# A gated recurrence with a mixer behind it: three of four batches loaded as whole tensors and computed in whole chunks

## The chip, the core and the metric

The kernel runs on one core of a Trainium2 chip. The metric is the time of one execution in device microseconds. Five engines work side by side, each through a queue of its own in the order in which the program wrote it: TensorE (PE in the profile; the loading of its weights is shown as PEld), VectorE (DVE), ScalarE (ACT), GpSimd (POOL) and SyncE (SP), which here issues all DMAs. An instruction that has to wait holds up what stands behind it on its engine.

## What is computed

The inputs are fp32: q, k, v and alpha of 4 batches, 8 heads, 768 tokens, 48 elements; U (768 x 32), V (32 x 768), w1 (384 x 1536) and w2 (1536 x 384). The output is 4 x 768 x 384 in fp32.

```
for t in range(S):                                   # S = 768, per batch and head
    state = alpha[t][:, None] * state + outer(k[t], v[t])
    y[t] = q[t] @ state
x = y, with the 8 heads side by side                 # 768 x 384 per batch
u = x + ((x.T @ U) @ V).T                            # low-rank mixing over tokens
out = u + relu(u @ w1) @ w2                          # MLP, 384 -> 1536 -> 384
```

## The kernel before

**The pieces.** Tokens are cut into chunks of C = 128, NC = 6 of them in a batch. In a chunk the decay is turned into sums of logarithms: ScalarE takes Ln of alpha (`lt`), TensorE sums it over the tokens by a triangular matrix, ScalarE takes exp of plus and minus the sum (`aa`, `ai`), q and k are multiplied by these (`rq`, `rk`) and transposed (`qT`, `kT`), and then the chunk's output is a masked product of scores (`pm`) with v (`rv`, a bf16 copy), plus q times the state (`st`) of the chunks before. A state update follows.

Two functions do this. `stage_gla` (L541) takes a chunk of 128 tokens with all 8 heads. `stage_pair` (L361) takes a block of 256 tokens with 4 heads: a partition holds two neighbouring tokens of each head, and the unit is done as two sub-chunks on halves of TensorE's rows. Either has six units in a batch. `PAIR = (0, 1, 2)` (L214) says which batches use pairs: the first three. In `stage_gla` the products `rq` and `rk` and the cast `rv` are given to GpSimd alone; in `stage_pair` the products may go to VectorE too, and the cast to ScalarE.

After a batch's six units comes `stage_mix` (L673: x.T U at L681, the residual's product with V at L712, transposes at L722), then the MLP: `mlp1` (first half, L749, two token halves of 12 tiles with three matmuls each) and `mlp2` (second half, L772, six chunks of 12 matmuls), whose sum is stored by SP (L780) from one of four `ou` buffers.

**The loads.** Each input of each unit has its own 192 KB tile from the pool `io`, with 36 slots (L261). A pair's tile is read in pieces of 2 x 48 elements, 384 B (L342), a chunk's in pieces of 48, 192 B (L349). w1 and w2 come in 12 tiles each through the same slots, and are cast to bf16 by GpSimd or ScalarE. A slot comes free when its reader is done.

**What sets the order.** All steps are entered with `P.add`: the engines that may do it and its cost on each in ns, what it reads and writes, and a key `prio`. `Plan.run` (L89) then walks through time by these costs. It takes, for an engine, the step that can start first, and among steps that can start at the same moment the one with the smallest key; it gives out the buffer slots as it goes, and writes each engine's queue in the resulting order. The chip runs the queues in this order whatever the steps really take. For a DMA the plan adds its cost to a common clock of the data, and lets SP run up to 3500 ns ahead of it; a pair load is entered with 750 ns, a chunk load with 1000, a weight tile with 540, a store with 550.

The keys of attention are 100 x (6 b + unit) and a little more, so 0, 600, 1200 and 1800 on for batches 0 to 3. The MLP's are 100 x (6 (b + 1) + 3 + 6 x), where x goes from 0 to 0.5 in the first half and from 0.5 to 1 in the second: 900 to 1500 for batch 0, 1500 to 2100 for batch 1. Loads have a unit's number 6 b + unit as their key, with offsets: alpha 0.7 earlier, v up to 1.25 later. U and V have 2.5, w1 5.5, w2 7.9 (`W2AT`).

Before the data come, TensorE is kept busy by `filler` matmuls (until 28 us of the plan).

Of the kernel before, what the change touches and what calls it, by code (L numbers as in the profile page):

```python
# [8 lines left out]
FP32 = mybir.dt.float32  # L9
BF16 = mybir.dt.bfloat16  # L10
AF = mybir.ActivationFunctionType
# [3 lines left out]
class Pool:  # L15

    def __init__(self, slots):
        self.slots = list(slots)
        self.free = [0.0] * len(self.slots)


class Buf:
# [10 lines left out]
    def __call__(self):  # L33
        return self.slot
# [140 lines left out]
def mm(*cols):  # L175
    return sum(max(c / 2.4 + 2.5, 25.0) for c in cols)
# [3 lines left out]
def kernel(  # L180
# [24 lines left out]

    const = ctx.enter_context(tc.tile_pool(name="const", bufs=1))
# [3 lines left out]
    def slots(name, n, shape, dtype):  # L210
        return [const.tile(shape, dtype, name=f"{name}{i}") for i in range(n)]

    W2AT = 7.9
    PAIR = (0, 1, 2)  # L214
    RES = (1, 1, 1, 0)
    P = Plan()
    nc.scalar.preload_act_table_set("natural_log_exp_and_others")

    u_in = const.tile([128, NC, R], FP32, name="u_in")
    v_in = const.tile([R, S], FP32, name="v_in")  # L220
    v_bf = const.tile([R, S], BF16, name="v_bf")
    u_sb = const.tile([128, NC, R], BF16, name="u_sb")
    vm_sb = const.tile([128, S], BF16, name="vm_sb")
# [23 lines left out]
    sel = const.tile([R, 4, R], BF16, name="sel")  # L247
# [10 lines left out]
    nc.vector.memset(offd[0:64, :, 1], -30000.0)  # L258
    nc.vector.memset(offd[64:128, :, 0], -30000.0)

    io = Pool(slots("io", 36, [C, H, D], FP32))  # L261
    lt_s = slots("lt", 3, [C, H, 64], BF16)
    rq_s = slots("rq", 3, [C, H, 64], BF16)
    rk_s = slots("rk", 4, [C, H, 64], BF16)
# [12 lines left out]
    pms = Pool(slots("pm", 3, [C, HP, 2, C], BF16))  # L277
    sms = Pool(slots("sm", 2, [128, DM], FP32))
    sts = Pool(slots("st", 4, [128, HP, 2 * D], BF16))
    xbs = Pool(slots("xb", 3, [128, NC, DM], BF16))  # L280
    ubs = Pool(slots("ub", 3, [128, NC, DM], BF16))
    utxs = Pool(slots("utx", 2, [128, DM], BF16))
    uts = Pool(slots("uT", 3, [128, NCT, S], BF16))
    h1s = Pool(slots("h1t", 2, [128, NJ, S], BF16))
    outs = Pool(slots("ou", 4, [C, DM], FP32))

# [9 lines left out]
    def copy(eng, dst, src):  # L296
        if eng == "ACT":
            nc.scalar.copy(dst, src)  # L298
        elif eng == "DVE":
            nc.vector.tensor_copy(dst, src)  # L300
        else:
            nc.gpsimd.tensor_copy(dst, src)  # L302

    def small():
        P.add({"SP": 450.0}, lambda e: nc.sync.dma_start(u_in, moe_U.rearrange("(c p) r -> p c r", p=128)), w=["u_in"], prio=2.5)
        P.add({"SP": 500.0}, lambda e: nc.sync.dma_start(v_in, moe_V), w=["v_in"], prio=2.5)
        P.add({"POOL": 300}, lambda e: nc.gpsimd.tensor_copy(u_sb, u_in), r=["u_in"], w=["u"], prio=395)
        P.add({"POOL": 800}, lambda e: nc.gpsimd.tensor_copy(v_bf, v_in), r=["v_in"], w=["v_bf"], prio=396)
        for i in range(2):
            vb = Buf(bank)  # L310
            sl = slice(i * TW, (i + 1) * TW)
            P.add({"PE": mm(TW)}, lambda e, vb=vb, sl=sl: nc.tensor.matmul(vb()[:, 0:TW], lhsT=sel.rearrange("r a b -> r (a b)"), rhs=v_bf[:, sl], start=True, stop=True), r=["v_bf"], w=[vb], prio=397, mode="V")
            P.add({"DVE": 470, "ACT": 390}, lambda e, vb=vb, sl=sl: copy(e, vm_sb[:, sl], vb()[:, 0:TW]), r=[vb], w=[("vm", i)], prio=398)

    def weight(dst, src, key, prio, pr, engs):
        t = Buf(io)
        P.add({"SP": 540.0}, lambda e: nc.sync.dma_start(flat(t), src), w=[t], prio=prio)  # L317
        P.add(engs, lambda e: copy(e, dst, flat(t)), r=[t], w=[key], prio=pr)

    def flat(t):  # L320
        return t().rearrange("p h d -> p (h d)")

    def weights1():
        for g in range(4):
            cs = slice(g * DM, (g + 1) * DM)
            for ct in range(NCT):
                weight(w1_sb[:, ct, cs], moe_w_ch1[ct * 128 : (ct + 1) * 128, cs], ("w1", g, ct), 5.5 + 0.01 * g, 560 + g, {"POOL": 485})
# [6 lines left out]
    tiles = {}  # L334

    def stage_loads(b):
        def load(t, src, c, key):
            if b in PAIR:
                hs, sl = slice((c % 2) * HP, (c % 2 + 1) * HP), slice((c // 2) * 2 * C, (c // 2 + 1) * 2 * C)
                P.add(  # L340
                    {"SP": 750.0},
                    lambda e: nc.sync.dma_start(  # L342
                        t().rearrange("p (h j) d -> p h (j d)", j=2), src[b, hs, sl, :].rearrange("h (p j) d -> p h (j d)", j=2)
                    ),
                    w=[t], prio=key,
                )
                return
            sl = slice(c * C, (c + 1) * C)
            P.add({"SP": 1000.0}, lambda e: nc.sync.dma_start(t(), src[b, :, sl, :].rearrange("h t d -> t h d")), w=[t], prio=key)  # L349

        for c in range(NC):
            at, qt, kt, vt = (Buf(io) for _ in range(4))
            tiles[b, c] = at, qt, kt, vt
            kk = b * NC + c
            for t, src, o in ((at, alpha, -0.7 if c else 0.0), (kt, k, 0.1), (qt, q, 0.2), (vt, v, 1.25 if c < NC - 1 and b in PAIR else 0.3)):
                load(t, src, c, kk + o)

    def xk(b, xb, c):
        return [(xb, c, 0), (xb, c, 1)] if b in PAIR else [(xb, c)]

    def stage_pair(b, u, sprev, xb):  # L361

        blk, half = u // 2, u % 2
        pr = (b * NC + u) * 100.0
        sl = 0.0 if b == 0 else 150.0
        at, qt, kt, vt = tiles[b, u]

        def raw(t):
            return t().rearrange("p (h j) d -> p j h d", j=2)

        def jh(x):
            return x.rearrange("p (j h) d -> p j h d", j=2)

        lt = Buf(lts)
        P.add({"ACT": 435}, lambda e: nc.scalar.activation(jh(lt()[:, :, 0:D]), raw(at), AF.Ln), r=[at], w=[lt], prio=pr + 40, slack=sl)  # L375
        rv = Buf(rvs)
        P.add({"POOL": 480, "ACT": 420}, lambda e: copy(e, jh(rv()), raw(vt)), r=[vt], w=[rv], prio=pr + 20, slack=sl)

        cb = Buf(bank)
        Q = HP * D  # L380
# [16 lines left out]
        aa, ai, tot = Buf(aas), Buf(ais), Buf(tots)  # L397
# [10 lines left out]
        P.add(both, lambda e: f_scale(e, rk, kt, ai), r=[kt, ai], w=[rk], prio=pr + 10, slack=sl)  # L408
        P.add(both, lambda e: f_scale(e, rq, qt, aa), r=[qt, aa], w=[rq], prio=pr + 11, slack=sl)

        tk, tq = Buf(bank), Buf(bank)
        kT, qT = Buf(kts), Buf(qts)
# [54 lines left out]
        def sview(x):  # L467
            return x[0]()[:, 2 * x[1] : 2 * x[1] + 2, :].rearrange("p a d -> p (a d)")
# [20 lines left out]
        for c in range(nch):  # L489
# [14 lines left out]
            else:  # L504
# [3 lines left out]
                    lambda e, c=c, sm=sm, prev=prev: nc.vector.tensor_tensor(sm()[:, 0:Q], db[c]()[:, 0:Q], sview(prev), op=ALU.add),  # L508
                    r=[db[c], prev], w=[sm], prio=pr + 4, slack=sl,
# [31 lines left out]
    def stage_gla(b, c, sprev, xb):  # L541
        kk = b * NC + c
        pr = kk * 100.0
        sl = 150.0
        at, qt, kt, vt = tiles[b, c]
        lt = Buf(lts)
        P.add({"ACT": 435}, lambda e: nc.scalar.activation(lt()[:, :, 0:D], at(), AF.Ln), r=[at], w=[lt], prio=pr + 40, slack=sl)
        rv = Buf(rvs)
        P.add({"POOL": 480}, lambda e: copy(e, rv(), vt()), r=[vt], w=[rv], prio=pr + 20, slack=sl)

        cb = Buf(bank)

# [11 lines left out]
        aa, ai, tot = Buf(aas), Buf(ais), Buf(tots)  # L564
# [10 lines left out]
        P.add(both, lambda e: f_scale(e, rk, kt, ai), r=[kt, ai], w=[rk], prio=pr + 10, slack=sl)  # L575
        P.add(both, lambda e: f_scale(e, rq, qt, aa), r=[qt, aa], w=[rq], prio=pr + 11, slack=sl)

        tk, tq = Buf(bank), Buf(bank)
        kT, qT = Buf(kts), Buf(qts)
# [41 lines left out]
        if c < NC - 1:  # L621
# [25 lines left out]
            else:  # L647
# [4 lines left out]
                    r=[db, sprev], w=[sm], prio=pr + 4, slack=sl,  # L652
# [112 lines left out]
    def mlp2(b, ub, h1, c):  # L765
# [13 lines left out]
        P.add({"DVE": 468}, lambda e: nc.vector.tensor_tensor(ou(), ub()[:, c, :], hb()[:, 0:DM], op=ALU.add), r=[hb, (ub, c)], w=[ou], prio=-100)  # L779
        P.add({"SP": 550.0}, lambda e: nc.sync.dma_start(out[b, c * C : (c + 1) * C, :], ou()), r=[ou], prio=-1)  # L780

    small()
    weights1()
    weights2()
    for b in range(B):
        stage_loads(b)
    for b in range(B):
        xb, ub, uT, h1 = Buf(xbs), Buf(ubs), Buf(uts), Buf(h1s)
        st = [None, None]
        for c in range(NC):  # L790
            if b in PAIR:
                st[c % 2] = stage_pair(b, c, st[c % 2], xb)
# [40 lines left out]
```

## Time and profile before

| What | Value |
| --- | --- |
| time, median of 3 runs | 176.6 us (176.31 to 178.05) |
| span of the profiled execution, first to last instruction | 175.2 us, clock of TensorE 1.000 |
| busy: PE, DVE, ACT, POOL | 165.0, 116.8, 104.9, 52.9 us |
| TensorE's largest groups | L749 53.5 us, L772 52.9 us, 288 matmuls each |
| HBM read, written | 23.79 MB, 4.72 MB |
| DMA packets under 512 B | 64,544 of 70,744 |
| waits of GpSimd's rv for v's loads | 21.5 us in 12 |

The time is that of an execution as a whole; the profile belongs to one execution, and its span leaves out what lies before the first and after the last instruction. Busy time of TensorE counts overlapping matmuls as they are modelled; where a part of its work is to be priced, the distance from one start to the next is the better measure. "Idle before" columns say what an engine waited for, and cost something only where the engine is the one that is late.

### The profile page before, as it was taken

To read this page: it belongs to the slowest core of one execution; us is meant where nothing else is said; L and a number is where in the kernel's file an instruction comes from. 1 tells how busy PE (TensorE), PEld (TensorE's weight loads), DVE (VectorE), ACT (ScalarE), POOL (GpSimd) and SP (SyncE) were. 2 spreads that over 40 slices of the span, in tenths; PEclk is the share of its full clock that TensorE was granted. 3 is DMA by queue.
4 is the path that set the end of the run, shared out by engine and by line. 5 is a ranking of instruction groups with operands and counts; after the bars stand their busy time and mean duration, and the time that the engine had idled before them with its cause. 6 is when DMAs were issued, how large, how long until landed. Compare 5 with 4: busy or idle time off the path is not lost.

```text
span 175.2 us, 5094 instructions
## 1 busy us (share of the span) xinstructions
PE 165.0 (94%) x1990; PEld 104.8 (60%) x1990; DVE 116.8 (67%) x251; ACT 104.9 (60%) x248; POOL 52.9 (30%) x92
## 2 busy tenths in 40 slices
PE   7788998699999999999999999999999999999992
PEld 2455665366566775766666666766666566666660
DVE  4588785398998889979888649987373385000321
ACT  4588874678788966457677434647784110996000
POOL 8055366258234432233243242920331000000000
PEclk9999999999999999999999999999999999999999
DMA  5999999999999999999698991021000212100222
GB/s 131 275 248 258 256 277 329 256 300 329 272 258 269 256 283 282 272 175 242 151 202 141 206 178 46 4 89 45 4 0 0 95 45 90 51 0 0 90 90 90
DMA packets 70744, 28.84 MB, mean 165 GB/s; under 512 B 64544, under 2 KB 70688, under 8 KB 70720
## 3 DMA queue, kind: packets, MB, share of 16 engines
q1 hardware_dynamic: 70720, 28.52, 67.2%
q8 instruction: 15, 0.25, 0.6%
q14 instruction: 9, 0.07, 0.2%
HBM read 23.79 MB, written 4.72 MB: 163 GB/s over the span
## 4 chain that ended last, share of the span: by engine, by line
PE 62%; SPq 14%; DMA 14%; POOL 4%; issue 3%; DVE 0%; POOLq 0%
PE ps L772 25%; PE ps L749 21%; SPq L342 11%; DMA io<-in_moe_w_ch_dram 6%; DMA io<-in_v_dram 5%; DMA io<-in_k_dram 3%; SPq L317 3%; POOL w_sb L302 2%; PE ps L418 2%; PE ps L712 2%; PE ps L722 2%; PE ps L584 2%; PE ps L531 1%; PE ps L445 1%; PE ps L605 1%
## 5 line engine op out<-in xcount | busy, mean ns | idle before, releaser
L749 PE MATMUL ps<-uT,w_sb 128*128 128x384 bf16 x288 | 53.5, 326 | 0.0
L772 PE MATMUL ps<-w_sb,h1t 128*128 128x384 bf16 x288 | 52.9, 326 | 0.0
L759 ACT ACTIVATE h1t<-ps 128x384 bf16<-128x384 f32 x70 | 33.9, 492 | 12.0 <-PE ps L749 11.9
L772 PEld LDWEIGHTS <-h1t 128*128 128x128 bf16 x288 | 26.1, 98 | 15.5 <-issue 0.6
L749 PEld LDWEIGHTS <-w_sb 128*128 128x128 bf16 x288 | 25.9, 98 | 15.4
L779 DVE TENSOR_TENSOR ou<-ub,ps 128x384 f32<-128x384 bf16 x24 | 13.2, 551 | 26.0 <-PE ps L772 25.8
L456 DVE TENSOR_TENSOR pm<-ps,maskp 128x512 bf16<-128x512 f32 x36 | 23.5, 682 | 2.8 <-PE ps L445 2.5
L761 DVE TENSOR_SCALAR h1t<-ps 128x384 bf16<-128x384 f32 x26 | 14.1, 553 | 7.6 <-PE ps L749 4.6
L302 POOL CAST rv<-io 128x384 bf16<-128x384 f32 x17 | 9.6, 567 | 28.2 <-DMA io<-in_v_dram 21.5
L298 ACT CAST xb<-ps 128x192 bf16<-128x192 f32 (+1 forms) x26 | 8.8, 353 | 10.3 <-PE ps L664 5.9
L298 ACT COPY qt<-ps 128x512 bf16<-128x512 bf16 x18 | 12.8, 709 | 3.5 <-PE ps L418 3.3
L375 ACT ACTIVATE lt<-io 128x384 bf16<-128x384 f32 x18 | 9.5, 527 | 8.3 <-DMA io<-in_alpha_dram 5.5
L713 DVE TENSOR_TENSOR ub<-xb,ps 128x384 bf16<-128x384 bf16 x24 | 12.0, 547 | 1.3 <-PE ps L712 1.3
L572 POOL TENSOR_TENSOR rk<-io,ai 128x384 bf16<-128x384 f32 x6 | 5.8, 970 | 22.6 <-ACT ai L565 22.6
L302 POOL CAST w_sb<-io 128x384 bf16<-128x384 f32 x21 | 10.6, 517 | 4.7 <-DMA io<-in_moe_w_ch_dram 4.4
L405 POOL TENSOR_TENSOR rk<-io,ai 128x384 bf16<-128x384 f32 x8 | 7.3, 915 | 11.6 <-ACT ai L398 10.8
L398 ACT ACTIVATE ai<-ps 128x384 bf16<-128x384 f32 x18 | 8.8, 487 | 2.1 <-PE ps L391 1.9
L298 ACT COPY kt<-ps 128x512 bf16<-128x512 bf16 x14 | 8.2, 583 | 1.8 <-PE ps L584 1.7
L615 DVE TENSOR_TENSOR pm<-ps,maskc 128x512 bf16<-128x512 f32 x12 | 7.9, 684 | 1.9 <-PE ps L605 1.8
L399 ACT ACTIVATE aa<-ps 128x384 bf16<-128x384 f32 x18 | 8.9, 493 | 0.0
L405 DVE TENSOR_TENSOR rk<-io,ai 128x384 bf16<-128x384 f32 x10 | 5.9, 588 | 4.1 <-ACT ai L398 4.1
L298 ACT COPY uT<-ps 128x768 bf16<-128x768 bf16 x4 | 3.2, 799 | 8.5 <-PE ps L722 8.3
(112 smaller groups left out, 256.8 us busy)
## 6 DMA issues: line engine op xcount, KB each, us to landing
io<-in_alpha_dram SPq DMA_DIRECT2D x24, 192.0 KB, 4.5
io<-in_k_dram SPq DMA_DIRECT2D x24, 192.0 KB, 4.5
io<-in_q_dram SPq DMA_DIRECT2D x24, 192.0 KB, 4.5
io<-in_v_dram SPq DMA_DIRECT2D x24, 192.0 KB, 4.6
io<-in_moe_w_ch_dram SPq DMA_DIRECT2D x24, 192.0 KB, 4.2
out_dram<-ou SPq DMA_DIRECT2D x24, 192.0 KB, 1.9
u_in<-in_moe_U_dram SPq DMA_DIRECT2D x1, 96.0 KB, 4.5
v_in<-in_moe_V_dram SPq DMA_DIRECT2D x1, 96.0 KB, 4.5
```

The lines of the kernel that those rows point to most:

```text
L298: nc.scalar.copy(dst, src)
L302: nc.gpsimd.tensor_copy(dst, src)
L342: lambda e: nc.sync.dma_start(t().rearrange("p (h j) d -> p h (j d)", j=2), src[b, hs, sl, :].rearrange("h (p j) d -> p h (j d)", j=2)),
L375: P.add({"ACT": 435}, lambda e: nc.scalar.activation(jh(lt()[:, :, 0:D]), raw(at), AF.Ln), r=[at], w=[lt], prio=pr + 40, slack=sl)
L405: eng.tensor_tensor(jh(dst()[:, :, 0:D]), raw(a), jh(x()), op=ALU.mult)
L456: nc.vector.tensor_tensor(dst, s2, maskp.to_broadcast([C, 2, 2, C]), op=ALU.mult)
L713: P.add({"DVE": 465}, lambda e, c=c, hb=hb: nc.vector.tensor_tensor(ub()[:, c, :], xb()[:, c, :], hb()[:, 0:DM], op=ALU.add), r=[hb] + xk( ...
L749: nc.tensor.matmul(hb()[:, 0:TW], lhsT=w1_sb[:, ct, jt * 128 : (jt + 1) * 128], rhs=uT()[:, ct, tt * TW : (tt + 1) * TW], start=(ct == 0), ...
L759: nc.scalar.activation(dst, hb()[:, 0:TW], AF.Relu)
L761: nc.vector.tensor_scalar_max(dst, hb()[:, 0:TW], 0.0)
L772: nc.tensor.matmul(hb()[:, 0:DM], lhsT=h1()[:, jt, c * C : (c + 1) * C], rhs=w2_sb[:, jt, :], start=(jt == 0), stop=(jt == NJ - 1),)
L779: P.add({"DVE": 468}, lambda e: nc.vector.tensor_tensor(ou(), ub()[:, c, :], hb()[:, 0:DM], op=ALU.add), r=[hb, (ub, c)], w=[ou], prio=-100)
```

## The change

Only batch 0 remains in pairs (`PAIR = (0,)`); batches 1, 2 and 3 go through `stage_gla`. For these three, each of alpha, k, q and v of a batch is loaded by one DMA of 1,179,648 B into a tile of 9216 B a partition, in which a partition holds head by head, and within a head the six chunks, one token of 48 elements each. A chunk reads every sixth row of it. The plan is given 4300 ns for such a load; the four have keys 6 b + 0.01 to 0.04.

The pool `io` is replaced by `bigs`, eight slots of 9216 B. Batch 0's loads, U, V and the weight tiles use sixths of such a slot (`Part`); a slot comes free when all that is in it has been read. V is loaded in two halves. The two tiles `u_in` and `v_in` are gone. `xb`, `ub` and `uT` have two buffers instead of three. Batch 0's loads are entered ahead of U and V; their keys stay.

```diff
-    PAIR = (0, 1, 2)
+    PAIR = (0,)
...
-    io = Pool(slots("io", 36, [C, H, D], FP32))
+    bigs = Pool(slots("big", 8, [C, NC * DM], FP32))
...
-    xbs = Pool(slots("xb", 3, [128, NC, DM], BF16))
-    ubs = Pool(slots("ub", 3, [128, NC, DM], BF16))
+    xbs = Pool(slots("xb", 2, [128, NC, DM], BF16))
+    ubs = Pool(slots("ub", 2, [128, NC, DM], BF16))
...
-    uts = Pool(slots("uT", 3, [128, NCT, S], BF16))
+    uts = Pool(slots("uT", 2, [128, NCT, S], BF16))
...
+    class Part:
+
+        def __init__(self):
+            if Part.used % NC == 0:
+                Part.big = Buf(bigs)
+            self.big, self.i = Part.big, Part.used % NC
+            self.key = (self.big, self.i)
+            Part.used += 1
+
+        def __call__(self):
+            return self.big()[:, self.i * DM : (self.i + 1) * DM]
+
+    Part.used = 0
+
+    class Chunk:
+
+        def __init__(self, big, c):
+            self.big, self.c, self.key = big, c, big
+
+        def __call__(self):
+            return self.big().rearrange("p (h c d) -> p h c d", h=H, c=NC)[:, :, self.c, :]
...
     def weight(dst, src, key, prio, pr, engs):
-        t = Buf(io)
-        P.add({"SP": 540.0}, lambda e: nc.sync.dma_start(flat(t), src), w=[t], prio=prio)
+        t = Part()
+        P.add({"SP": 540.0}, lambda e: nc.sync.dma_start(t(), src), w=[t.key], prio=prio)
...
+        def whole(t, src, key):
+            P.add(
+                {"SP": 4300.0},
+                lambda e: nc.sync.dma_start(
+                    t().rearrange("p (h c d) -> p h c d", h=H, c=NC), src[b].rearrange("h (c p) d -> p h c d", p=C)
+                ),
+                w=[t], prio=key,
+            )
+
+        if b in PAIR:
+            for c in range(NC):
+                kk = b * NC + c
+                tiles[b, c] = [None] * 4
+                for i, src, o in ((0, alpha, -0.7 if c else 0.0), (2, k, 0.1), (1, q, 0.2), (3, v, 1.25 if c < NC - 1 else 0.3)):
+                    t = Part()
+                    tiles[b, c][i] = t
+                    load(t, src, c, kk + o)
+            return
+        bb = []
+        for i, src in ((0, alpha), (2, k), (1, q), (3, v)):
+            bb.append((i, Buf(bigs)))
+            whole(bb[-1][1], src, b * NC + 0.01 * len(bb))
+        bb = dict(bb)
         for c in range(NC):
-            at, qt, kt, vt = (Buf(io) for _ in range(4))
-            tiles[b, c] = at, qt, kt, vt
...
+            tiles[b, c] = [Chunk(bb[i], c) for i in range(4)]
...
+    stage_loads(0)
     small()
+    Part.used += -Part.used % NC
     weights1()
     weights2()
-    for b in range(B):
+    for b in range(1, B):
         stage_loads(b)
```

More of the change, by code (lines that the diff above doesn't have):

```diff
@@ L219 @@
     u_in = const.tile([128, NC, R], FP32, name="u_in")
-    v_in = const.tile([R, S], FP32, name="v_in")
     v_bf = const.tile([R, S], BF16, name="v_bf")
@@ L302, in copy @@
             nc.gpsimd.tensor_copy(dst, src)
-    def small():
[L305 to L308, printed above, removed]
+    class Part:
[13 more added lines that the diff above has]
+            return self.big().rearrange("p (h c d) -> p h c d", h=H, c=NC)[:, :, self.c, :]
+    def small():
+        ui, vi = Part(), Part()
+        vj = Part()
+        v2 = [vi, vj]
+        P.add({"SP": 450.0}, lambda e: nc.sync.dma_start(ui()[:, 0 : NC * R].rearrange("p (c r) -> p c r", c=NC), moe_U.rearrange("(c p) r -> p c r", p=128)), w=[ui.key], prio=2.5)
+        P.add({"POOL": 300}, lambda e: nc.gpsimd.tensor_copy(u_sb, ui()[:, 0 : NC * R].rearrange("p (c r) -> p c r", c=NC)), r=[ui.key], w=["u"], prio=395)
         for i in range(2):
@@ L311, in small @@
             sl = slice(i * TW, (i + 1) * TW)
-            P.add({"PE": mm(TW)}, lambda e, vb=vb, sl=sl: nc.tensor.matmul(vb()[:, 0:TW], lhsT=sel.rearrange("r a b -> r (a b)"), rhs=v_bf[:, sl], start=True, stop=True), r=["v_bf"], w=[vb], prio=397, mode="V")
+            P.add({"SP": 250.0}, lambda e, i=i, sl=sl: nc.sync.dma_start(v2[i]()[0:R, 0:TW], moe_V[:, sl]), w=[v2[i].key], prio=2.5)
+            P.add({"POOL": 400}, lambda e, i=i, sl=sl: nc.gpsimd.tensor_copy(v_bf[:, sl], v2[i]()[0:R, 0:TW]), r=[v2[i].key], w=[("v_bf", i)], prio=396)
+            P.add({"PE": mm(TW)}, lambda e, vb=vb, sl=sl: nc.tensor.matmul(vb()[:, 0:TW], lhsT=sel.rearrange("r a b -> r (a b)"), rhs=v_bf[:, sl], start=True, stop=True), r=[("v_bf", i)], w=[vb], prio=397, mode="V")
             P.add({"DVE": 470, "ACT": 390}, lambda e, vb=vb, sl=sl: copy(e, vm_sb[:, sl], vb()[:, 0:TW]), r=[vb], w=[("vm", i)], prio=398)
     def weight(dst, src, key, prio, pr, engs):
-        t = Buf(io)
-        P.add({"SP": 540.0}, lambda e: nc.sync.dma_start(flat(t), src), w=[t], prio=prio)
-        P.add(engs, lambda e: copy(e, dst, flat(t)), r=[t], w=[key], prio=pr)
-    def flat(t):
-        return t().rearrange("p h d -> p (h d)")
+        t = Part()
+        P.add({"SP": 540.0}, lambda e: nc.sync.dma_start(t(), src), w=[t.key], prio=prio)
+        P.add(engs, lambda e: copy(e, dst, t()), r=[t.key], w=[key], prio=pr)
     def weights1():
@@ L337, in load @@
         def load(t, src, c, key):
[L338 to L347, printed above, removed]
@@ L348, in load @@
-            sl = slice(c * C, (c + 1) * C)
-            P.add({"SP": 1000.0}, lambda e: nc.sync.dma_start(t(), src[b, :, sl, :].rearrange("h t d -> t h d")), w=[t], prio=key)
-        for c in range(NC):
-            at, qt, kt, vt = (Buf(io) for _ in range(4))
-            tiles[b, c] = at, qt, kt, vt
-            kk = b * NC + c
-            for t, src, o in ((at, alpha, -0.7 if c else 0.0), (kt, k, 0.1), (qt, q, 0.2), (vt, v, 1.25 if c < NC - 1 and b in PAIR else 0.3)):
-                load(t, src, c, kk + o)
+            hs, sl = slice((c % 2) * HP, (c % 2 + 1) * HP), slice((c // 2) * 2 * C, (c // 2 + 1) * 2 * C)
@@ new lines, in load @@
+            P.add(
+                {"SP": 750.0},
+                lambda e: nc.sync.dma_start(
+                    t().rearrange("p (h j) -> p h j", j=2 * D), src[b, hs, sl, :].rearrange("h (p j) d -> p h (j d)", j=2)
+                ),
+                w=[t.key], prio=key,
+            )
+        def whole(t, src, key):
+            P.add(
+                {"SP": 4300.0},
+                lambda e: nc.sync.dma_start(
+                    t().rearrange("p (h c d) -> p h c d", h=H, c=NC), src[b].rearrange("h (c p) d -> p h c d", p=C)
+                ),
+                w=[t], prio=key,
+            )
@@ L368, in raw @@
         def raw(t):
-            return t().rearrange("p (h j) d -> p j h d", j=2)
+            return t().rearrange("p (h j d) -> p j h d", j=2, d=D)
         def jh(x):
@@ L374, in stage_pair @@
         lt = Buf(lts)
-        P.add({"ACT": 435}, lambda e: nc.scalar.activation(jh(lt()[:, :, 0:D]), raw(at), AF.Ln), r=[at], w=[lt], prio=pr + 40, slack=sl)
+        P.add({"ACT": 435}, lambda e: nc.scalar.activation(jh(lt()[:, :, 0:D]), raw(at), AF.Ln), r=[at.key], w=[lt], prio=pr + 40, slack=sl)
         rv = Buf(rvs)
-        P.add({"POOL": 480, "ACT": 420}, lambda e: copy(e, jh(rv()), raw(vt)), r=[vt], w=[rv], prio=pr + 20, slack=sl)
+        P.add({"POOL": 480, "ACT": 420}, lambda e: copy(e, jh(rv()), raw(vt)), r=[vt.key], w=[rv], prio=pr + 20, slack=sl)
         cb = Buf(bank)
@@ L407, in stage_pair @@
         both = {"DVE": 420, "POOL": 885}
-        P.add(both, lambda e: f_scale(e, rk, kt, ai), r=[kt, ai], w=[rk], prio=pr + 10, slack=sl)
-        P.add(both, lambda e: f_scale(e, rq, qt, aa), r=[qt, aa], w=[rq], prio=pr + 11, slack=sl)
+        P.add(both, lambda e: f_scale(e, rk, kt, ai), r=[kt.key, ai], w=[rk], prio=pr + 10, slack=sl)
+        P.add(both, lambda e: f_scale(e, rq, qt, aa), r=[qt.key, aa], w=[rq], prio=pr + 11, slack=sl)
         tk, tq = Buf(bank), Buf(bank)
@@ L546, in stage_gla @@
         lt = Buf(lts)
-        P.add({"ACT": 435}, lambda e: nc.scalar.activation(lt()[:, :, 0:D], at(), AF.Ln), r=[at], w=[lt], prio=pr + 40, slack=sl)
+        P.add({"ACT": 435}, lambda e: nc.scalar.activation(lt()[:, :, 0:D], at(), AF.Ln), r=[at.key], w=[lt], prio=pr + 40, slack=sl)
         rv = Buf(rvs)
-        P.add({"POOL": 480}, lambda e: copy(e, rv(), vt()), r=[vt], w=[rv], prio=pr + 20, slack=sl)
+        P.add({"POOL": 480}, lambda e: copy(e, rv(), vt()), r=[vt.key], w=[rv], prio=pr + 20, slack=sl)
         cb = Buf(bank)
@@ L574, in stage_gla @@
         both = {"POOL": 885}
-        P.add(both, lambda e: f_scale(e, rk, kt, ai), r=[kt, ai], w=[rk], prio=pr + 10, slack=sl)
-        P.add(both, lambda e: f_scale(e, rq, qt, aa), r=[qt, aa], w=[rq], prio=pr + 11, slack=sl)
+        P.add(both, lambda e: f_scale(e, rk, kt, ai), r=[kt.key, ai], w=[rk], prio=pr + 10, slack=sl)
+        P.add(both, lambda e: f_scale(e, rq, qt, aa), r=[qt.key, aa], w=[rq], prio=pr + 11, slack=sl)
         tk, tq = Buf(bank), Buf(bank)
```

## The prediction

> **What bounds the kernel now.** I read the busy time by stretches first, because the share of TensorE over the whole span mixes a start that waits for data with a rest that does not. Its columns are the stretch, its length, the busy time of PE, PEld, DVE, ACT and POOL, then the granted clock, the DMA share and GB/s.
>
> ```profile
> 0.00:33.00 33.00, 26.77 (x412) 16.66 (x413) 22.27 (x62) 21.46 (x52) 16.93 (x40) 1.00 1.03 252
> 33.00:172.00 139.00, 138.24 (x1581) 88.14 (x1578) 94.15 (x189) 83.48 (x198) 35.98 (x52) 1.00 0.61 146
> ...
> 46.00:56.00 10.00, 9.69 (x160) 6.16 (x158) 9.53 (x25) 8.06 (x22) 2.65 (x5) 1.00 1.16 263
> ...
> 97.00:100.00 3.00, 3.00 (x38) 1.75 (x37) 1.56 (x3) 1.18 (x3) 0.25 (x1) 1.00 1.31 203
> ```
>
> From 33 us to 172 us TensorE is idle for 0.8 us of 139, at full clock: it is the bound there. Before 33 us the DMAs are (252 GB/s, while TensorE waits). The last two rows compare loads: 46 to 56 us moves pieces of 384 B (two tokens of a head side by side, L342) at 263 GB/s; 97 to 100 us moves only the fourth batch, in pieces of 192 B (one token, L349), at 203 GB/s. The SP queue in that second stretch shows that the loads, not the issuer, set this rate (start, duration, line):
>
> ```profile
> 95.67 0.72 SPq L349 DMA_DIRECT2D io<-in_v_dram  x1
> 96.45 0.69 SPq L349 DMA_DIRECT2D io<-in_alpha_dram  x1
> 97.24 0.98 SPq L349 DMA_DIRECT2D io<-in_k_dram  x1
> 98.31 0.92 SPq L349 DMA_DIRECT2D io<-in_q_dram  x1
> 99.32 1.10 SPq L349 DMA_DIRECT2D io<-in_v_dram  x1
> ```
>
> The same instruction takes 0.38 us when the queue is empty (the shortest alpha and k issues); here they follow each other and grow to about 1 us. 196,608 B at 203 GB/s are 0.97 us, so they are held back at the pace of the data.
>
> **What TensorE saves.** Two batches go from token pairs (`stage_pair`) to whole chunks (`stage_gla`). I priced a unit from start to next start in TensorE's timeline, since busy times overlap. A pair unit of the third batch:
>
> ```profile
> 81.78 0.33 PE L518 MATMUL ps<-st,qt 128*128 128x96 bf16 x4
> 82.04 0.37 PE L531 MATMUL ps<-rv,pm 64*128 64x48 bf16 x16
> 82.35 1.15 PE L749 MATMUL ps<-uT,w_sb 128*128 128x384 bf16 x6
> 83.43 0.34 PE L479 MATMUL ps<-rv,rk 64*128 64x96 bf16 x8
> 83.71 0.40 PE L418 MATMUL ps<-ident,rk 128*128 128x128 bf16 x4
> 83.94 0.39 PE L418 MATMUL ps<-ident,rq 128*128 128x128 bf16 x4
> 84.16 1.63 PE L749 MATMUL ps<-uT,w_sb 128*128 128x384 bf16 x9
> ```
>
> and a chunk unit of the fourth:
>
> ```profile
> 117.73 0.33 PE L628 MATMUL ps<-rv,rk 128*128 128x96 bf16 x4
> 117.90 0.65 PE L749 MATMUL ps<-uT,w_sb 128*128 128x384 bf16 x3
> 118.38 0.39 PE L584 MATMUL ps<-ident,rk 128*128 128x128 bf16 x4
> 118.61 0.39 PE L584 MATMUL ps<-ident,rq 128*128 128x128 bf16 x4
> 118.83 0.65 PE L749 MATMUL ps<-uT,w_sb 128*128 128x384 bf16 x3
> 119.32 0.33 PE L662 MATMUL ps<-st,qt 128*128 128x96 bf16 x4
> 119.49 0.36 PE L664 MATMUL ps<-rv,pm 128*128 128x48 bf16 x8
> 119.69 0.65 PE L749 MATMUL ps<-uT,w_sb 128*128 128x384 bf16 x3
> ```
>
> Pair: state times q 0.26, scores times v 0.31, state update 0.28, transposes 0.45; with the scores (L445, 85.72 to 86.07) 0.35 and the sums (L384 on, 86.57 to 87.03) 0.46 that is 2.11 us, and 12.5 a batch (two first units have half of the state product, 0.18). Chunk: update 0.17, transposes 0.45, state product 0.17, scores times v 0.20, scores (L605, 120.27 to 120.60) 0.33, sums (L554 on, 124.40 to 124.69) 0.29: 1.61 us, 9.3 a batch (update and state product are there five times). Two batches save 2 x 3.2 = **6.4 us of TensorE**. The 139 us after 33 become 132.6.
>
> **What the loads cost.** No whole-tensor load is in the trace. Its pieces are still one token of one head, 192 B, 48 a partition instead of 8; the nearest row is the 203 GB/s above: 1,179,648 B take 5.8 us. From the other side, the 263 GB/s of the 384 B pieces would make it 4.5 us. I take 5.8, as the length of a piece is what the two rows differ in and the length is that of the slow row; 4.5 stays as the other end. A batch then takes 23.2 us (or 18) to arrive, where a pair batch takes 4.72 MB / 263 GB/s = 18.
>
> The Trainium skill ("DMA: Bandwidth & Descriptors", section "Rules for kernel authors") asks for DMAs of 1 MiB and more, and its table of measurements gives 341 GB/s at 1 MB; by that a whole tensor would take an estimated 3.5 us and the change would win. The row speaks against applying it here: with five loads queued back to back the data still came at 203 GB/s, so the number of loads was not what held them.
>
> **When the data are there.** Batch 0 (4.72 MB), U and V (0.20) and w1 (2.36) are 7.28 MB. 252 GB/s for 33 us is 8.32 MB, so the 1.04 MB beyond took 4 us and those 7.28 MB were in at 29 us. The first batch, U, V and w1 keep their order and sizes (V in two halves: 0 to 1 us of SP, taken as 0, under the backlog). Behind w1 the SP queue now has four whole tensors of batch 1 (keys 6.01 to 6.04) and only then w2 (key 7.9); before, w2 came after eight pieces of batch 1. All eight `big` slots suffice for this: four of batch 0, one small, two of w1, one free, and the early ones come back while w1 loads. So batch 1 is through at 29 + 23.2 = 52.2, and landed some 1.7 us later (an unhurried store shows 1.9 from issue to landing) at 53.9; w2 (12 in 6.55 us, L317) at 52.2 to 58.8. Batch 2: 58.8 + 23.2 + six stores of batch 0 at 0.55 = 85.3. Batch 3: another 26.5, 111.8, landed about 113.5.
>
> **What of it is on the path.** At 33.1 us TensorE has left of the first MLP half of batch 0: 66 matmuls of 0.163 us, 10.7 us. With the residual's L712 (0.8) and, for the three chunks that the lt, ai and aa slots let ahead, sums 0.9, transposes 1.35 and scores 1.0, it has 14.8 us: until 48. The next work needs v (54) or the first cast w2 tile (52.2 + 0.55 + 1.7 + 0.5 = 55). **First stall: 6 us**, which alone gives back the 6.4.
>
> Then the order matters. Each engine runs its queue in the order that `Plan.run` wrote, and the plan takes 4300 ns for a whole tensor, 1.5 us less than my row. Over eight loads it believes the data to be there 12 us too soon, over twelve 18. It therefore puts batch 2's attention (keys from 1200) ahead of the first MLP half of batch 1 (from 1500), and batch 3's (from 1800) ahead of the second half (1800 to 2100): TensorE waits there with MLP work behind it. What stands behind batch 3's first transposes: second MLP half of batch 1 11.7 (72 matmuls of 0.163), attention 9.3, mixing 2.5 (L681 0.43, L712 1.0, L722 1.0), and two MLPs of 23.4: 70.3; I take off 4 for MLP pieces that fill the chunk's own latencies: 66. Batch 3's v is landed at 113.5; POOL has the casts of up to five chunks (0.505 each, L302) and rk (0.914, L572) before it: 117. The present order adds about 3% of gaps: by starts there are 570 MLP matmuls of 0.163 after 33 us (92.7), attention 12.5 + 12.5 + 9.3 and mixing 8.3 (three batches of 2.5 and the 0.8), 135 in 139. So 66 x 1.03 = 68, end of TensorE 185, and 3.2 for the last sum and store (172 to 175.2): span 188. From batch 2's side: v at 85.3 + 0.6, behind it 92.3 us (attention 9.3 less the 1.5 that needs no v, mixing 2.5, MLP 23.4, then batch 3's 11.8 and two MLPs of 23.4), x 1.03 and + 3.2: 184. I take the middle, a span of 186. The executions take 1.4 us more than the span (176.6 to 175.2): **187 us**, beside the profiled execution's own 175.2 and the median 176.6 alike.
>
> **The smaller edits.** Nothing each, with what covers it. Reads of a chunk now step over the tensor: Ln on stepped pairs takes 527 ns and on plain chunks 523. DVE's rk and rq (0.588 each) go to POOL (0.914), where two products and the cast make 2.33 us a chunk, so POOL has at most 52.9 + 12 x 2.33 = 81 us of work in 175; on a batch's first chunk it is counted above. Two instead of three xb, ub and uT: batch 3's residual needs batch 1's second MLP half done, which ends near 117 us now, against its own L712 at 141; if that cover shrinks, up to 2 us. Stores behind a whole load wait up to 5.8 us; four `ou` slots cover about 12 us of second MLP half (3 us each with what is mixed in); without that cover, 0 to 6 us more. SP's 60 saved issues are worth nothing, as it waited for room anyway.
>
> **The rivals.** *The loads are quick.* If 48 rows a partition run at the pace of the pair loads, 4.5 us a tensor, batch 1 is landed at 48.7, w2 soon after, the plan's belief is nearly right, and only 1.5 us of the first stall is left: 33 + 132.6 + 1.5 + 3.2 = 170.3, time **172 us**. For it speaks that 203 GB/s is one short stretch with TensorE busy; against, that 4 us at 88 show the same 201. Between 4.5 us (172) and 5.8 (187) an equal time lies near 4.9 us a tensor (241 GB/s): this decides the sign. *The order swallows the lateness.* If MLP work stands ahead of batches 2 and 3 where they are late, only the first stall of 6 us and up to 3 of others remain: 33 + 132.6 + 6 + 3 + 3.2, a time near **178-179 us**. Present attention and MLP interleave at that grain; against it speaks that the plan has no reason to wait for data that it believes landed. *The change does nothing to the bound* would need the chunk form to cost as much TensorE as the pair form; the starts above exclude it.
>
> **How the numbers follow.** Slow loads with stalls 0.60 (182 to 193), quick loads 0.27 (169 to 175), swallowed 0.13 (175 to 181). One measurement tells about 1% here (176.3 to 178.1 in three runs), so faster is 0.27, within 1% half of the swallowed case, 0.07, and slower 0.66. The range leaves out the best half of the quick case and the worst tip of the slow one: 171 to 192; the likeliest case's own range is 182 to 193.
>
> **What would show it.** Right: about 200 GB/s from 30 us to 110, SP's whole-tensor issues of nearly 6 us each, TensorE below 8 tenths near 48 to 55 us and again near 75 to 87 and 105 to 117, with POOL's rv and rk waiting for v and k. Wrong: loads near 4.5 us each, or an idle TensorE after 33 us of under 3 us in all. A TensorE with fewer than 6 us saved in L384 to L531 would make the first term wrong.

## The result

| | median | runs | profiled execution: time, span |
| --- | --- | --- | --- |
| before | 176.84 us | 176.31 to 178.05 | span 175.2 us |
| changed | 198.63 us | 197.32 to 200.43 | 199.09 us, span 197.3 us |

The changed kernel takes 1.119 times the time (95% interval 1.112 to 1.125); by the medians it is 21.8 us more. Ratios here and below leave out executions over 1.5% above the fastest of their kernel, as the one of 200.43 us. The sign of the forecast was right and its size was not: 187 us was forecast, and the range ended at 192.

First TensorE and the loads by stretches, in the columns of the prediction's first view:

```profile
33.00:194.00 161.00, 138.06 (x1332) 87.70 (x1330) 85.76 (x162) 80.40 (x191) 45.50 (x61) 0.97 0.57 127
...
36.00:60.00 24.00, 16.94 (x193) 11.16 (x191) 13.04 (x26) 15.50 (x39) 11.80 (x17) 0.97 1.01 224
64.00:92.00 28.00, 19.71 (x219) 12.54 (x218) 16.80 (x34) 9.33 (x24) 8.21 (x11) 1.00 0.89 182
92.00:112.00 20.00, 18.08 (x207) 11.90 (x205) 13.90 (x25) 14.85 (x36) 7.74 (x11) 1.00 0.97 193
112.00:128.00 16.00, 10.42 (x90) 5.82 (x87) 5.43 (x10) 2.90 (x7) 4.05 (x7) 0.79 0.49 99
128.00:194.00 66.00, 65.90 (x573) 41.57 (x570) 31.46 (x60) 32.41 (x73) 10.42 (x12) 1.00 0.13 46
```

Before, TensorE lacked 0.8 us in 139. Now it lacks 23 in 161: 7 while batch 1 comes in, 8 at batch 2 (64 to 92), 2 more, and 6 at batch 3 (112 to 128). After 128 us it is as full as before. The seventh number behind the stretch is new too: the granted clock, 1.00 throughout the profiled execution before, is 0.79 in the stretch of the last wait. The loads themselves, in the SP queue (start, duration, line):

```profile
27.50 7.40 SPq L371 DMA_DIRECT2D big<-in_k_dram  x1
35.36 5.62 SPq L371 DMA_DIRECT2D big<-in_q_dram  x1
41.45 6.23 SPq L371 DMA_DIRECT2D big<-in_v_dram  x1
47.78 10.84 SPq L341 DMA_DIRECT2D big<-in_moe_w_ch_dram  x12
...
104.85 6.26 SPq L371 DMA_DIRECT2D big<-in_v_dram  x1
```

From q to v and from v to w2 it is 6.1 and 6.3 us: a whole tensor takes 6.2 us, not 5.8 and far from 4.3. The last one, issued from 104.85 to 111.11, lands only at 119: the end of an issue is not the landing. What happens there stands in GpSimd's timeline and, below it, TensorE's:

```profile
110.25 0.91 POOL L608 TENSOR_TENSOR rq<-big,aa 128x384 bf16<-128x384 f32 x1
119.36 1.86 POOL L301 CAST rv<-big 128x384 bf16<-128x384 f32 x4 [8.20 <-DMA big<-in_v_dram]
121.18 0.91 POOL L608 TENSOR_TENSOR rk<-big,ai 128x384 bf16<-128x384 f32 x1
```

```profile
122.15 0.50 PE L664 MATMUL ps<-rv,rk 128*128 128x96 bf16 x4 [5.58 <-POOL rk L608]
122.45 0.63 PE L620 MATMUL ps<-ident,rk 128*128 128x128 bf16 x4
123.02 0.61 PE L620 MATMUL ps<-ident,rq 128*128 128x128 bf16 x4
123.41 1.49 PE L808 MATMUL ps<-w_sb,h1t 128*128 128x384 bf16 x4
124.83 0.82 PE L717 MATMUL ps<-xb,u_sb 128*32 128x384 bf16 x6
```

GpSimd waits 8.2 us for batch 3's v, casts four chunks of it, and only then makes the first chunk's rk; TensorE stands still for 5.6 us before that, with second-half matmuls of batch 1's MLP (L808) written behind it. They need nothing that is late. Four of them then take 1.49 us instead of the 0.81 that four took before the wait. Behind them comes batch 2's mixing (L717), still undone at this point.

### The profile page after: what moved, and what is told of

The parts are those of the page before. It is cut to its first block, busy times and chain, and to the rows that moved or that the text cites. A ratio compares the mean times of both kernels' runs of the same rounds, so it can differ in the third digit from the quotient of the medians.

```text
span 197.3 us, 4428 instructions
## 1 busy us (share of the span) xinstructions
PE 165.9 (84%) x1738; PEld 105.2 (53%) x1738; DVE 108.1 (55%) x221; ACT 100.3 (51%) x237; POOL 64.2 (33%) x104
## 4 chain that ended last, share of the span: by engine, by line
PE 41%; DMA 30%; SPq 11%; POOL 7%; issue 6%; ACT 2%; DVE 2%; POOLq 0%; ACTq 0%
PE ps L808 17%; DMA big<-in_k_dram 16%; PE ps L785 15%; DMA big<-in_v_dram 10%; SPq L362 8%; DMA big<-in_moe_w_ch_dram 4%; POOL rk L608 3%; PE ps L620 2%; SPq L341 1%; POOL w_sb L301 1%; PE ps L641 1%; POOL rv L301 1%; PE ps L664 1%; PE ps L758 1%; PE ps L748 1%
## 5 line engine op out<-in xcount | busy, mean ns | idle before, releaser
L808 PE MATMUL ps<-w_sb,h1t 128*128 128x384 bf16 x288 | 54.0, 331 | 0.0
L808 PEld LDWEIGHTS <-h1t 128*128 128x128 bf16 x288 | 26.5, 99 | 15.9 <-issue 1.2
L608 POOL TENSOR_TENSOR rk<-big,ai 128x384 bf16<-128x384 f32 x18 | 16.6, 930 | 43.2 <-ACT ai L601 21.9
L651 DVE TENSOR_TENSOR pm<-ps,maskc 128x512 bf16<-128x512 f32 x36 | 23.3, 683 | 4.8 <-PE ps L641 4.8
L301 POOL CAST rv<-big 128x384 bf16<-128x384 f32 x23 | 11.5, 523 | 25.1 <-DMA big<-in_v_dram 16.4
L608 POOL TENSOR_TENSOR rq<-big,aa 128x384 bf16<-128x384 f32 x18 | 16.2, 912 | 7.7 <-DMA big<-in_q_dram 7.7
L297 ACT CAST xb<-ps 128x384 bf16<-128x384 f32 (+1 forms) x22 | 9.6, 436 | 13.2 <-PE ps L700 10.5
L583 ACT ACTIVATE lt<-big 128x384 bf16<-128x384 f32 x18 | 8.8, 532 | 12.8 <-DMA big<-in_alpha_dram 6.1
L664 PE MATMUL ps<-rv,rk 128*128 128x96 bf16 x60 | 5.3, 218 | 8.1 <-POOL rk L608 7.5
L620 PE MATMUL ps<-ident,rq 128*128 128x128 bf16 x72 | 7.2, 225 | 4.2 <-POOL rq L608 4.0
L620 PE MATMUL ps<-ident,rk 128*128 128x128 bf16 x72 | 7.5, 230 | 3.5 <-POOL rk L608 3.5
L700 PE MATMUL ps<-rv,pm 128*128 128x48 bf16 x144 | 6.8, 187 | 3.4 <-POOL rv L301 3.4
```

Source lines behind the costliest of these rows:

```text
L620: nc.tensor.matmul(t[:, p, :], lhsT=ring()[:, 2 * p : 2 * p + 2, :].rearrange("t h w -> t (h w)"), rhs=ident, start=True, stop=True, is_tr ...
L651: nc.vector.tensor_tensor(pm()[:, :, par, :], s2, maskc.to_broadcast([C, HP, C]), op=ALU.mult)
L808: nc.tensor.matmul(hb()[:, 0:DM], lhsT=h1()[:, jt, c * C : (c + 1) * C], rhs=w2_sb[:, jt, :], start=(jt == 0), stop=(jt == NJ - 1),)
```

## The experiments

Three theories were set against each other. **O**: the written order believes the data to be there earlier than they are, as the plan takes 4300 ns for a load that takes 6200. **R**: the loads are slow, and no order helps. **S**: loads stand behind stores on SP, which wait for TensorE, which waits for loads. A fourth came out of the runs: **W**, that a whole tensor holds back a batch's first chunk, whatever its pace and the order.

### The order alone: e1

```diff
-                {"SP": 4300.0},
+                {"SP": 6100.0},
```

> The changed kernel with one number altered: the plan takes 6100 ns for a whole-tensor load instead of 4300, which is the pace of those loads in the trace of the changed kernel (issues of k, q and v of batch 1 start 27.5, 35.4 and 41.5 us). Loads, work and buffers are the same; only the written order changes. Theory O (the order believes the data to be early, so TensorE's queue waits with MLP work behind it): the stalls at batches 2 and 3 go, the first stall of about 6 us stays; TensorE idle after 33 us falls from 23 us to 8-11, time 184 to 187. Theory R (192 B pieces are simply too slow, whatever the order): idle stays above 18 us and the time above 194.

185.98 us, 1.048 times before (1.042 to 1.053): 12.6 us of the 21.8 are gone with one number, and no load is faster. Stretches of this kernel:

```profile
36.00:60.00 24.00, 20.04 (x203) 13.12 (x200) 16.41 (x33) 15.89 (x40) 12.30 (x17) 0.82 1.03 223
64.00:92.00 28.00, 27.28 (x288) 17.22 (x285) 18.24 (x36) 17.04 (x42) 11.03 (x13) 1.00 0.92 196
...
112.00:128.00 16.00, 14.91 (x161) 9.58 (x160) 11.23 (x22) 5.10 (x12) 8.88 (x14) 1.00 0.58 139
```

The hole at batch 2 falls from 8.3 to 0.7 us and that at batch 3 from 5.6 to 1.1, while the casts of batch 3's v start at the same moment, 118.6 (119.4 in the change). O is shown for these two. The first hole stays: 4 us idle now instead of 7, but the clock is at 0.82 over the 24 us, which is up to 4.3 us of full speed.

### Stores on another queue: e2

```diff
-nc.sync.dma_start(out[b, c * C : (c + 1) * C, :], ou())
+nc.scalar.dma_start(out[b, c * C : (c + 1) * C, :], ou())
```

> The changed kernel with the 24 result stores issued from ScalarE's queue instead of SP's; the written order of all else is the same. Theory S (loads stand behind stores on SP, and the stores wait for TensorE, which waits for loads): v of batch 2 is issued near 74 us instead of 82.3, v of batch 3 near 95 instead of 104.9, TensorE idle after 33 us falls by 8 us or more and the time to 188-191. Theory O alone: the loads are late by their own pace, the data of batch 3 come at best 6 us earlier, time 192-194 or, if ScalarE is held by its waiting stores, no gain: 196-200.

196.07 us, 1.104 (1.097 to 1.111). In the profiled execution (198.5 us) batch 2's v is issued at 76.0 instead of 82.3 us, as S expects, but batch 3's at 104.6, where it was 104.9: what SP loses behind stores it makes up later, as the loads run at their own pace anyway. S is worth about 2.6 us.

### w2 ahead of batch 1: e3, and with the corrected cost: e5

```diff
-    W2AT = 7.9
+    W2AT = 5.7
```

> The changed kernel with the key of w2 lowered from 7.9 to 5.7, so that w2 is loaded before batch 1 instead of after it. The second MLP half of batch 0 then has its weights at 37 us and covers the wait for batch 1; batch 1 lands 6.6 us later. If the first stall (between 36 and 60 us, 7 us idle) is a loss of its own, the time falls to 190-193. If the time is set by when batch 3 lands and by what stands behind it (O and S), it hardly moves, 195-199, as the sum of loads ahead of batch 3 is the same.

199.03 us, 1.122 (1.115 to 1.129): nothing, as its second answer has it. e5 has this and the 6100 ns together.

> The changed kernel with both the plan's cost of a whole load at 6100 and w2 loaded before batch 1. By starts TensorE has 26.4 us of work without batch 1 (both MLP halves of batch 0), so that it lasts from 33 to about 60 us, and batch 1's v lands near 61; batch 2 near 89, with 32 us of work from 61 on; batch 3 near 117. Theory O (with a right order the data are only just late): idle after 33 us below 6 us, time 174 to 178. If the pace of the loads alone sets the end, it stays where the corrected cost left it, 184 to 187.

186.56 us, 1.050 (1.044 to 1.057): nothing either, against the 186.0 of e1. The expectation of 174 to 178 was a miss; the time lies in the band of the other answer, though it is not the pace of the loads alone that keeps it there, as e9 below shows with the same pace at 180.0. The expectation counted TensorE's work up to batch 1's landing and then took batch 1's MLP as ready; but the MLP needs all six chunks and the mixing, and these cannot start before the fourth tensor is in. Covering the wait for the data only moved the hole to 64 to 80 us, where batch 1's chunks run one after the other:

```profile
64.00:72.00 8.00, 5.69 (x90) 4.45 (x87) 7.05 (x13) 4.41 (x11) 4.93 (x8) 0.79 0.94 209
72.00:80.00 8.00, 5.53 (x78) 3.44 (x76) 5.70 (x12) 4.42 (x15) 1.62 (x3) 1.00 0.93 196
```

### The length of the pieces: e4, and with the plan's costs right: e10

Batches 1 and 2 stay whole tensors, but in pieces of 384 B, computed by `stage_pair`:

```diff
+        def wide(t, src, key):
...
+                    t().rearrange("p (h k x) -> p h k x", h=H, k=NC // 2), src[b].rearrange("h (k p j) d -> p h k (j d)", p=C, j=2)
...
-            whole(bb[-1][1], src, b * NC + 0.01 * len(bb))
+            (wide if b in WIDE else whole)(bb[-1][1], src, b * NC + 0.01 * len(bb))
```

> The changed kernel with batches 1 and 2 still loaded as whole tensors, but in pieces of 384 B (two tokens side by side) and computed by the pair function; batch 3 as in the change. It asks whether the length of the pieces or the whole tensor as such sets the pace. If the piece: 4.5 us a tensor (263 GB/s) for eight of the twelve loads, so that the plan's 4300 is right for them, and the 6.4 us of TensorE are not saved: time 178-182. If a whole-tensor load is slow as such: still near 6 us each, and with the pair function's dearer TensorE 198-204.

190.99 us, 1.078 (1.072 to 1.084). The rate, while batch 1's whole tensors come in:

```profile
30.00:46.00 16.00, 14.33 (x128) 9.43 (x129) 10.61 (x19) 11.96 (x31) 4.03 (x5) 1.00 1.03 259
```

259 GB/s, where the change has 192 between 30 and 56 us. With the prediction's rows (263 and 203 GB/s for single chunks) that makes four cases: the length of the piece sets the pace here, whole tensor or not. That part of R is shown. But the time is far above the 178-182 that this pace should have given. e10 repeats it with 4600 ns for these loads and 6100 for batch 3's:

> The kernel with batches 1 and 2 as whole tensors in pieces of 384 B and computed in pairs, now with the plan's costs at the measured pace: 4600 ns for these and 6100 for the whole tensors of batch 3. If the loss of 14 us that it still had is the false belief about batch 3 (its issues stood behind stores at 71 to 95 us and TensorE waited at 96 to 112), the time falls to 178-182. If whole tensors cost by holding back a batch's first chunk, at whatever pace, it stays at 186 or more.

185.02 us, 1.043 (1.036 to 1.051), nearly on the figure of the second answer. With quick loads and a right order, 7 us are still missing. They lie where TensorE does batch 1's units in a row:

```profile
48.00:64.00 16.00, 13.16 (x240) 8.69 (x239) 13.32 (x32) 11.37 (x28) 6.03 (x11) 0.68 0.90 260
```

It is idle for 2.8 us, and 16 us at 0.68 of the clock are up to 5.1 us of full speed less. That is W; by these numbers the clock is the larger part of it here.

### The same computing with a DMA for each chunk: e6 and e9

e6 is the kernel before with one edit; e9 is the change with its whole loads cut into six, where a chunk waits for its own piece alone.

```diff
-    PAIR = (0, 1, 2)
+    PAIR = (0,)
```

> The kernel before with only the first batch in pairs: batches 1, 2 and 3 in whole chunks, each chunk's input loaded by its own DMA in 192 B pieces (planned at 1000 ns, as the fourth batch is before), three xb, ub and uT. It has the change's computing and its piece length, without the whole tensors, and its loads are spread by need, with w2 after nine pieces of batch 1. If the pace of 192 B pieces is what costs, 72 loads of 0.97 us end near 29 + 70 + 7 + 6 = 112 us and the time is 182 or more. If the whole tensor and the plan's belief cost it (all four must be there before the first chunk; 4300), the 6.4 us of TensorE are mostly kept: 170 to 176.

176.57 us, 0.9955 (0.992 to 0.999). The loads are the slow 192 B pieces and end no earlier than in the change: the last v is issued at

```profile
113.81 0.99 SPq L349 DMA_DIRECT2D io<-in_q_dram  x1
114.90 0.93 SPq L349 DMA_DIRECT2D io<-in_v_dram  x1
```

and 10 us later than there. R as a whole falls: with the slow pace and this computing the time is that of the kernel before. But the pace is not free:

```profile
33.00:171.70 138.70, 133.99 (x1327) 85.46 (x1324) 83.50 (x160) 78.60 (x185) 48.60 (x65) 1.00 0.75 149
```

TensorE is busy for 4.2 us less than before, and idle for 4.7 us instead of 0.8. Of the 6.4 us that were to be saved, 0.9 are seen in the time.

```diff
-            self.big, self.c, self.key = big, c, big
+            self.big, self.c, self.key = big, c, (big, c // 1)
...
-        def whole(t, src, key):
+        def piece(t, src, g, key):
+            cs = slice(g * 1, (g + 1) * 1)
             P.add(
-                {"SP": 4300.0},
+                {"SP": 1000.0},
...
-                w=[t], prio=key,
+                w=[(t, g)], prio=key,
...
-            whole(bb[-1][1], src, b * NC + 0.01 * len(bb))
+            for g in range(6):
+                piece(bb[-1][1], src, g, b * NC + g * 1 + 0.01 * len(bb))
```

> The changed kernel, everything as it is (slots of 9216 B, V in halves, two buffers, whole-chunk computing), except that each whole-tensor load is cut into six loads of one chunk into the same slot, planned at 1000 ns each with the chunk's own key; a chunk waits for its own pieces alone. If it is the whole tensor that costs (no chunk of a batch can start before 23 us of loads are through, and the order was written for 4300), the time is that of the kernel with chunk loads from its own tiles, 176 to 178. If slots, V or the order of the first batch cost, it stays above 181.

179.97 us, 1.014 (1.007 to 1.021): 18.7 of the 21.8 us belong to the whole tensors, order and grain together; against e1, which has a right order too, the grain alone is 6.0. The time lies 2 us above the expected band, and the 3.4 us to e6 are not taken apart further: the shared slots, V in halves, the order of the first batch and the stepped destination are all in them.

### The buffers: e8

```diff
-    xbs = Pool(slots("xb", 3, [128, NC, DM], BF16))
+    xbs = Pool(slots("xb", 2, [128, NC, DM], BF16))
```

and the same for `ub` and `uT`, in the kernel before.

> The kernel before with two instead of three buffers for xb, ub and uT, the change's buffer part alone. Every theory says no difference, 176 to 178; more than 1.8 us would make the buffers a cause of the change's loss.

177.32 us, 1.001 (0.998 to 1.005). No cause.

### Which batch: e11 and e12, and a faster kernel: e7

e11 is the change with batch 1 in pairs and pieces too, and 6100 ns for the rest; e12 has the 4300.

```diff
-    PAIR = (0,)
+    PAIR = (0, 1)
```

> The changed kernel with batch 1 in pairs too, loaded piece by piece like batch 0 (into sixths of the slots), and batches 2 and 3 as whole tensors with the plan's cost at 6100. It asks where the rest goes that the corrected cost left (186 against 180 with chunk pieces). If it is batch 1 alone, because nothing but batch 0's MLP (23.4 us) is there to cover 25 us of loading and then six chunks in a row, it is gone: 174 to 178. If every whole batch costs its share, two thirds of it stay: 181 to 184.

178.09 us, 1.000 (0.997 to 1.004). The 8 us that e1 had left are gone, though batch 1's pairs cost TensorE 3.2 us more again: W is in the main a matter of batch 1. e11 alters grain, pace and computing of that batch at once; that it is the grain follows from e9 (180.0 with slow pieces) and e10 (185.0 with quick whole tensors).

> The same with the plan's cost left at 4300. The belief is then wrong by eight loads instead of twelve, 8 x 1.9 = 15 us too early at batch 3 instead of 23. If TensorE's wait follows that lateness, the loss against the corrected cost is about two thirds of the 12.6 us that it was for three batches: 8 us, a time of 183 to 187.

192.82 us, 1.091 (1.083 to 1.098). The false belief costs 14.7 us with two whole batches, where 8 were expected, and no less than the 12.6 with three: it does not add up load by load. Its trace has waits at both batches: TensorE is idle for 5.8 us between 64 and 96, at a clock of 0.89, and for 2.8 between 112 and 128, where here too GpSimd casts four chunks of batch 3's v (111.8 us) before the first rk. Why it is not less than with three batches stays open.

e7 is the kernel before with `PAIR = (0, 1)`, each chunk of batches 2 and 3 with its own loads.

> The kernel before with batches 0 and 1 in pairs and 2 and 3 in whole chunks with their own 192 B loads. Loads up to w2 and batch 1 are as before. TensorE saves 3.2 us in batch 2; its loads take 24 x 0.97 = 23 us instead of 18. If TensorE stays the bound: 173 to 174.5. If the slower loads come late: 177 or more.

174.36 us, 0.983 (0.976 to 0.989): faster than both kernels, by about 2% against before. It keeps the 3.2 us of TensorE, with batch 1 in the quick pieces.

### What the runs say together

How far TensorE is when batch 3's v comes in tells the cases apart. The second column is the time of a cast of batch 3's v in GpSimd's timeline (the first casts for whole tensors, the last for chunk loads), the third the span less that:

| kernel | cast of v | from there to the end | time |
| --- | --- | --- | --- |
| change | 119.4 | 77.9 us | 198.6 |
| e1, cost 6100 | 118.6 | 64.8 us | 186.0 |
| e9, chunk loads in the same slots | 121.0 | 57.3 us | 180.0 |
| e6, chunk loads | 118.7 | 56.2 us | 176.6 |

The last data come at 119 to 121 us in all four. What differs is how much TensorE still has to do then: 336, 320, 284 and 282 matmuls of the MLPs and 274, 188, 130 and 125 others, from the change down to e6. In the change batch 2's mixing and batch 3's chunks are among them, and a wait of 2.8 us comes first. Grain and order of the loads decide this.

## Why the prediction was right in its sign and wrong in its size

The mechanism was foreseen: loads that come late, and an order that makes TensorE wait for them in front of MLP work. What failed are terms of the sum for batch 3: when its v lands (113.5 forecast, 119.4 measured), how long TensorE goes on from there (71.5 forecast, 74.6 measured), and the mean that was taken where the later side binds. One part of the mechanism was missed as well, the grain (W). Term by term:

- **"Two batches save 6.4 us of TensorE"**: stands as far as it was tried. e7, with one batch changed and its data in time, is 3.1 us faster than before (177.4 to 174.4), against 3.2 counted from starts. For two batches no run shows it: e6 gains 0.9.
- **"1,179,648 B take 5.8 us"**: right in kind, 7% short. The chip took 6.2, and e4 shows the row that it was read from to be the right one, the length of the piece. Over twelve loads this is 5 us. The first casts of v come at 56.0, 90.8 and 119.4 us for the three batches, where the sum has 53.9, 85.9 and "landed about 113.5". Of the 11.3 us between the forecast span of 186 and the 197.3 measured, this is 5.9.
- **"First stall: 6 us"**: 7 us of idle time were measured between 36 and 60 us. What the term left out is that a batch's chunks, once all data are there, run in a row with little beside them: with a right order and w2 early (e5) the hole is still there, later. It was priced as waiting for data alone; a missing overlap of loading and computing within a batch comes with it, and e11 shows the two together to be worth 8 us net at batch 1.
- **"The order matters"**: right, and the largest part, 12.6 us by e1. The chain foreseen, casts of v on GpSimd ahead of rk and TensorE in front of it with MLP behind, is the one in the trace.
- **"What stands behind batch 3's first transposes ... 66 x 1.03 = 68"**: short by 3. From v's landing to the last matmul there were 74.6 us (119.4 to 194), where the sum had 71.5 (113.5 to 185). Six of them ran at about 0.6 of the clock (122 to 128 us), a loss of 2.5 us that no term had. Batch 2's mixing, 2.5 us by the prediction's own price, was still to do (L717 above), and the term has only batch 3's.
- **"I take the middle, a span of 186"**: a mistake of its own. Of the two sides (184 from batch 2, 188 from batch 3) the later one binds, as both are waits in one queue; a mean has no mechanism behind it. That is 2 us; with 5.9 and 3.1 it makes 11.0 of the 11.3.
- **The rivals.** "The loads are quick" is out: 4.5 us would have needed longer pieces. "The order swallows the lateness" (178-179) did not happen in the change; e11 comes to such a time, but with a right cost and batch 1 in pairs. The point at which the sign turns, 4.9 us a tensor, was not tried with the change's computing. e10, with 4.5 us for eight of twelve loads, is 7.4 us slower than before; its pairs do not save the 6.4, but even less these it would not be faster, as that sum had no term for the grain. The rule of the Trainium skill ("DMA: Bandwidth & Descriptors", section "Rules for kernel authors") that a DMA should have 1 MiB or more brought nothing with pieces of 192 B: 192 GB/s at 1.18 MB a DMA against 203 at 0.2 MB. The 3.5 us that the prediction estimates from that page rest on a table of DMAs issued from GpSimd; these are issued from SP and took 6.2.
- **The range** ended at 192, and its slow case had 5.8 us a tensor throughout. The row behind it is 3 us long, and single microseconds of it show 186 to 216 GB/s; 6.2 us (190 GB/s) lay within that.

## What to carry to other kernels

Count a load's grain as well as its rate: if a batch's first chunk cannot be finished before the batch's last load is in, loading and computing of that batch hardly overlap, and what covers the gap must already be there; at the start of a pipeline little is. Where the order is written out from assumed costs, one wrong cost of a DMA puts late work ahead of ready work on every queue that it touches; set it from the trace before judging the change. When several waits bound an end, take the latest of them.

## What the hardware showed that was not expected

**Packets of four pieces.** The page of the changed kernel says of its packets:

```profile
DMA packets 39108, 28.78 MB, mean 146 GB/s; under 512 B 14448, under 2 KB 39088, under 8 KB 39088
```

Before, 64,544 of 70,744 were under 512 B. Now 24,640 lie between 512 B and 2 KB; less the 48 weight and store tiles of 128 rows and the 64 rows of V, 18,432 belong to the twelve whole loads, 768 B each, which is four pieces of 192 B. Four times fewer packets than 192 B each would make, and the rate did not rise (192 GB/s against 203).

**The clock.** It was 1.000 in the profiled execution of the kernel before (0.977 to 1.000 in others) and is 0.97 over the change between 33 and 194 us, 5 us of full speed by that figure. The Trainium skill ("TensorE: Matmul & The Clock Gate", section "Part 1: The HAM clock gate") says that an idle TensorE is put to half rate and needs about 3.4 us of work to come back. The trace shows such a fall at the wait of 5.6 us, and the slow matmuls end near 127, some 5 us after it. In e1 it lasts longer: one wait of 2.95 us at 48 to 51 us, and the following small matmuls stay at the slow spacing (0.54 us for four transposes instead of 0.22) up to 61 us although no wait of over 0.5 us is among them. By the granted clock the fall is up to 4.3 us of full speed in e1 (24 us at 0.82) and 5.1 in e10, and 1.7 in e9 (28 us at 0.94). It seems to be a good part of what W costs, 6.0 us from e1 to e9 and 7.4 from e10 to the kernel before, but no run takes it away by itself.
